# Attention with routed experts and a dense layer: who copies the transposed probabilities while 64-bit words are converted, and when the words are ordered

## Chip, core and metric

The kernel runs on one core of a Trainium2 chip. The metric is the device time of one execution in microseconds (us); the smaller the better. Engines: TensorE (PE, its weight loads PEld), VectorE (DVE), ScalarE (ACT), GpSimd (POOL), SyncE (SP), which only issues transfers here.

## What is computed

```python
# q, k, v: (2, 8, 768, 64); 16 cluster centroids per head
mask   = argmax(q_n @ c_n.T)[:, :, :, None] == argmax(k_n @ c_n.T)[:, :, None, :]
scores = where(mask, q @ k.T / 8, -1e9)
attn   = softmax(scores)                      # 768 x 768 per head, 16 heads
x      = (attn @ v) as rows of 1536 tokens x 512
e      = argmax(x @ w_gate + modality_bias[modality_id])     # 8 experts
x      = gate * (relu(x @ w1[e]) @ w2[e])     # 512 -> 1024 -> 512
out    = softplus(x @ w_in) @ w_out           # 512 -> 2048 -> 512
```

`w_in` and `w_out` arrive as float64, that is as pairs of 32-bit words; the kernel makes float32 of them itself.

## The kernel before

**Three stages.** Attention fills the first 300 us, the experts follow up to about 465 us, the dense layer (`g`, `o`) takes the rest. The change lies in the attention stage.

**Attention steps.** 16 heads of 6 row tiles make 96 steps, numbered `g`; the loop over `g` near line 1090 issues every step in the same order, and each engine works through its own instructions in that order. Step `g` is software-pipelined over three neighbours:

- `av_step(g)`: PE multiplies the transposed probabilities of the head before by `v` (tile `av`, L356).
- `S_mm(g+2)`: PE computes the scores of step g+2 (tile `S`, two buffers, L305 and L320); DVE takes their negated row maximum (`nm`, L322).
- `P_T(g)`: PE transposes the probabilities `P` of step g in six 128x128 blocks (L344) into two PSUM tiles `Tp` (i = 0 and 1; two buffers in all). Each `Tp` is copied to `PT` in SBUF: i = 1 always by ACT (L349), i = 0 by DVE (L347) or ACT.
- then the `jobs` of the step: loads (`load_raw`, `load_v`, `cv_load`), cluster masks (`sims_*`, tiles `sim`, `simT`, `mk`), the end of a head (`fin_x`, `fin_l`).
- `S_exp(g+2)`: ACT computes `P = exp(S + nm)` and its row sum (L331). This frees the `S` buffer.
- then the `after` work of the step (conversion, below), and a quarter of the split of a coming head's q and k (`prep_part`: ACT `kA` L278 and `qA` L283, DVE `kB` L281 and `qA` L286, POOL). `put_mask` sends mask rows into `qB` and `kB` by eight small transfers (L296).

**Conversion of the 64-bit words.** 16 pieces, j = 0 to 15, of 1 MB. `cvg[j] = 11 + (19*j)//4` is the step at which piece j begins: 11, 15, 20, 25, 30, 34, 39, 44, 49, 53, 58, 63, 68, 72, 77, 82. `cv_load(j)` (L439) brings the words into tile `words`, of which there are two buffers, so piece j can only land when piece j-2 has been read for the last time. At step cvg[j] ACT takes the absolute value of the high words (`cvd<-words`, L452); in the three steps behind it DVE does the rest: L454 and L455, then L460, then L464, which is the last reader of `words`. `cv_store(j)` (L470) writes the result to `w_rows` at step cvg[j]+4.

**SP's order.** All these transfers are issued by SP, one behind the other: a transfer that must wait for a buffer holds up those behind it. `load_raw` (L174, L175) brings q and k of a coming pair of heads and has to wait until DVE's `qA` of an earlier pair (L286) is done.

**What the diff touches:** the set `busy` (the three steps behind each cvg[j], 48 in all), the condition in `P_T`, and the step at which `cv_load` is issued.

```python
job(g0 - 4, cv_load, j)
for k in range(4):
    after.setdefault(g0 + k, []).append((cv_bits, (j, k)))
    if k:
        busy.add(g0 + k)
```

Of the kernel before, what the change touches and what calls it, by code (L numbers as in the profile page):

```python
# [32 lines left out]
def body(ctx, tc, qT, kT, vP, cen, mod, wg, bias, w1, w2, win, wout, out):  # L33
# [114 lines left out]
    desc = p_1.tile([128, 16], F32, name="desc")  # L148
    mk_a = p_1.tile([128, 1], F32, name="mk_a")
    mk_b = p_1.tile([128, 1], F32, name="mk_b")  # L150
    busy = set()
    raw, vt, sims, spl, mks, PT, P_t, S_t, nm_t, sums, av_t, xTu, rec, xb, lgT = ({} for _ in range(15))

    pend = []
# [181 lines left out]
    def P_T(g):  # L336
        h, t = divmod(g, NT)
        if t == 0:
            PT[h] = p_PT.tile([128, NT, S], F32, tag="PT", name="PT")
        P = P_t.pop(g)  # L340
        for i in range(2):
            ps = ps_T.tile([128, 3, 128], F32, tag="t", name="Tp")
            for j in range(3):
                pe.transpose(ps[:, j, :], P[:, i, j * 128:(j + 1) * 128], ident)  # L344
            dst = PT[h][:, 3 * i:3 * i + 3, t * 128:(t + 1) * 128]
            if i == 0 and g not in busy:
                dve.tensor_copy(dst, ps)  # L347
            else:
                act.copy(dst, ps)  # L349
# [595 lines left out]
    with tc.manual_schedule():  # L945
# [54 lines left out]
        def job(g, f, *a):  # L1000
            jobs.setdefault(g, []).append((f, a))
# [17 lines left out]
            job(6 * h + 14, fin_l, h)  # L1019
            job(6 * h + 15, fin_lT, h)  # L1020

        cvg = [11 + (19 * j) // 4 for j in range(16)]
        for j in range(16):
            g0 = cvg[j]
            job(g0 - 4, cv_load, j)
            for k in range(4):
                after.setdefault(g0 + k, []).append((cv_bits, (j, k)))
                if k:
                    busy.add(g0 + k)
            after.setdefault(g0 + 4, []).append((cv_store, (j,)))  # L1030

        e_t = p_1.tile([128, LROWS // 128 * LW], U32, name="empty")
# [60 lines left out]
        for g in range(NH * NT):  # L1093
            h, t = divmod(g, NT)
            if g > NT:
                av_step(g)
            S_mm(g + 2)
            P_T(g)
            for f, a in jobs.get(g, ()):
                if inspect.isgeneratorfunction(f):  # L1100
                    run(f, *a)
                else:
                    f(*a)
            S_exp(g + 2)
            drain()
            for f, a in after.get(g, ()):
                f(*a)
            h2, i2 = divmod(g - 3, NT)
            h2 += 2
            if 2 <= h2 < NH and i2 < 4:  # L1110
                prep_part(h2, i2)
                if i2 == 0 and h2 > 2:
                    put_mask(h2)
            if g == 8:
                put_mask(2)
# [64 lines left out]
        for i in range(1, LF + 1):  # L1180
            k = i - 1
# [13 lines left out]
        for x in seq:  # L1195
            kd, k, w, h = x
# [38 lines left out]
        for n in range(1, end):  # L1235
            kd, k, w, h = seq[n]
# [8 lines left out]
            while ks < len(halves) and at_load.get(halves[ks], end) < n + (n == 1):  # L1245
                k = halves[ks]
# [171 lines left out]
        for n in range(2, end):  # L1418
            kind, i, layer, s = seq[n]
# [153 lines left out]
        for c, y in enumerate((ys[NM - 1][1], ps_A.tile([128, 512], F32, tag="a", name="o"))):  # L1573
            cs = slice(c * 256, c * 256 + 256)
            for kt in range(16):
                gh, gl = gs[NM - 1, kt // 4]
                hi, lo = wts["out", kt // 2]
                a, k = (kt % 4) * 256 + 128, (kt % 2) * 512 + c * 256
# [50 lines left out]
```

## Time and profile before

| | |
|---|---|
| median of 3 runs | 746.4 us (745.55 to 747.06) |
| the profiled execution | 748.49 us, its span 746.8 us |
| busy over the span | PE 703.2, PEld 562.5, DVE 457.7, ACT 392.3, POOL 160.7 us |
| DMA | 100.18 MB, 134 GB/s on average |

The span is what the trace covers, and all times in trace rows count from its start; the remaining 1.7 us lie around it. Busy time is the sum of an engine's instructions; a row of the timeline gives the start, the duration, the engine, the line, the tile written `<-` the tiles read, and in brackets for how long the engine had been idle and what released it.

### The profile page before, as it was taken

How to read it: one execution, taken by the hardware profiler on the slowest of the kernel's cores; microseconds unless marked ns; L12 is line 12 of the kernel's file. 1: busy time of each engine (PE TensorE's matmuls, PEld its weight loads, DVE VectorE, ACT ScalarE, POOL GpSimd, SP SyncE). 2: the span in 40 equal slices, each digit the busy share in tenths (PEclk: the TensorE clock that was granted, in tenths of full speed). 3: DMA queues.
4: the chain of work that ended last, by engine and by line, in shares of the span. 5: the costliest groups of instructions: out<-in, count | busy, mean ns of one | idle time of the engine just before them, and what ended most of it. 6: DMA issues, size and time to landing. Idle time of an engine off the chain costs nothing. (4 is left out here: it accounts for less than half of the span.)

```text
span 746.8 us, 11746 instructions
## 1 busy us (share of the span) xinstructions
PE 703.2 (94%) x4498; PEld 562.5 (75%) x4498; DVE 457.7 (61%) x668; ACT 392.3 (53%) x635; POOL 160.7 (22%) x172
## 2 busy tenths in 40 slices
PE   4898999899888999999999999989999999999998
PEld 2665665556455655888898878989889899899887
DVE  4898998799799985865747446684423424323220
ACT  3777886787687876344645535542332332322320
POOL 4501120111231203664362431260000000000000
PEclk9999999999999999999999999999999999999999
DMA  4407354534534525769868964301000100000000
GB/s 136 148 17 257 112 208 145 204 135 160 201 123 145 178 104 183 250 227 397 324 228 310 411 216 168 128 1 29 26 18 15 37 7 29 1 1 29 1 29 28
DMA packets 38683, 100.18 MB, mean 134 GB/s; under 512 B 7934, under 2 KB 15486, under 8 KB 36576
## 3 DMA queue, kind: packets, MB, share of 16 engines
q1 hardware_dynamic: 35888, 92.22, 35.3%
q0 software_dynamic: 2592, 6.79, 2.6%
q8 instruction: 36, 0.59, 0.3%
q10 hardware_dynamic: 144, 0.39, 0.2%
q14 instruction: 23, 0.19, 0.1%
HBM read 79.13 MB, written 19.17 MB: 132 GB/s over the span
## 5 line engine op out<-in xcount | busy, mean ns | idle before, releaser
L1508 DVE SCALAR_TENSOR_TENSOR sp<-g,sp 128x1024 f32<-128x1024 f32 x24 | 29.4, 1224 | 149.7 <-ACT sp L1507 149.7
L1497 PE MATMUL g<-xh,wh 128*128 128x256 f32 x384 | 109.1, 284 | 0.0
L1497 PE MATMUL g<-xl,wh 128*128 128x256 f32 x384 | 108.1, 281 | 0.0
L1497 PE MATMUL g<-xh,wl 128*128 128x256 f32 x384 | 108.0, 281 | 0.0
L331 ACT ACTIVATE P<-S,nm 128x768 f32<-128x768 f32 x96 | 87.0, 906 | 38.8 <-DVE nm L322 34.7
L344 PE MATMUL Tp<-ident,P 128*128 128x128 f32 x576 | 84.7, 280 | 15.3 <-ACT PT L349 9.7
L1505 ACT ACTIVATE sp<-g 128x1024 f32<-128x1024 f32 x24 | 24.6, 1027 | 137.5 <-PE g L1497 127.6
L322 DVE TENSOR_REDUCE nm<-S 128x1 f32<-128x768 f32 x96 | 90.7, 946 | 9.1 <-PE S L320 8.7
L344 PEld LDWEIGHTS Tp<-ident,P 128*128 128x128 f32 x576 | 68.0, 142 | 28.5 <-ACT PT L349 15.2
L742 POOL TENSOR_TENSOR wl<-raw,wh 128x1024 fp32r<-128x1024 f32 x22 | 54.2, 2475 | 131.1 <-ACT wh L741 124.1
L356 PE MATMUL av<-PT,v 128*64 128x384 f32 x384 | 78.9, 506 | 0.0
L742 DVE TENSOR_TENSOR wl<-raw,wh 128x1024 fp32r<-128x1024 f32 x50 | 66.1, 1362 | 13.1 <-ACT wh L741 13.1
L741 ACT CAST wh<-raw 128x1024 fp32r<-128x1024 f32 x69 | 69.0, 1050 | 9.8 <-DMA raw<-in_w 7.2
L1497 PEld LDWEIGHTS g<-xl,wh 128*128 128x128 f32 x384 | 73.5, 191 | 0.5
L1497 PEld LDWEIGHTS g<-xh,wh 128*128 128x128 f32 x384 | 73.4, 191 | 0.5
L1497 PEld LDWEIGHTS g<-xh,wl 128*128 128x128 f32 x384 | 73.3, 191 | 0.0
L349 ACT COPY PT<-Tp 128x384 f32<-128x384 f32 x144 | 64.2, 483 | 14.9 <-PE Tp L344 14.1
L1532 PE MATMUL o<-wh,gT 128*128 128x512 f32 x216 | 69.7, 394 | 0.0
L305 PEld LDWEIGHTS S<-kA,qA 128*128 128x128 f32 x192 | 29.9, 195 | 50.2 <-ACT P L331 13.9
L305 PE MATMUL S<-kA,qA 128*128 128x384 f32 x192 | 60.6, 399 | 4.2 <-ACT P L331 3.8
L844 PE MATMUL y<-wh,hT 128*128 128x512 f32 x192 | 63.1, 398 | 0.0
L819 PE MATMUL h<-xh,wh 128*128 128x256 f32 x192 | 55.0, 287 | 0.5 <-DVEq L1350 0.5
(284 smaller groups left out, 1403.9 us busy)
## 6 DMA issues: line engine op xcount, KB each, us to landing
raw<-in_w SPq DMA_DIRECT2D x56, 512.0 KB, 7.5
words<-in_win SPq DMA_DIRECT2D x8, 1024.0 KB, 5.5
w_rows<-cvt SPq DMA_DIRECT2D x16, 512.0 KB, 3.2
words<-in_wout SPq DMA_DIRECT2D x8, 1024.0 KB, 6.5
whole<-in_w SPq DMA_DIRECT2D x16, 512.0 KB, 6.9
raw<-w_rows SPq DMA_DIRECT2D x16, 512.0 KB, 5.0
rawq<-in_qT SPq DMA_DIRECT2D x8, 384.0 KB, 3.6
v<-in_vP SPq DMA_DIRECT2D x8, 384.0 KB, 4.7
```

Source lines behind the costliest of these rows:

```text
L305: pe.matmul(ps[:, i, :HS], qA[:, t * 128:t * 128 + 128], kA[:, i * HS:(i + 1) * HS], start=True, stop=False)
L322: dve.tensor_reduce(out=nm_t[g], in_=ps[:, :, :HS], axis=AX.XY, op=ALU.max, negate=True)
L331: act.activation(out=P_t[g], in_=S_t.pop(g)[:, :, :HS], func=AF.Exp, bias=nm_t.pop(g), scale=1.0, accum_out=sums[h][:, t:t + 1],)
L344: pe.transpose(ps[:, j, :], P[:, i, j * 128:(j + 1) * 128], ident)
L349: act.copy(dst, ps)
L356: pe.matmul(av_t[h][64 * a:64 * a + 64, :], vt[p][:, kt, 64 * i:64 * i + 64], PT[h][:, kt, a * HS:(a + 1) * HS], start=(kt == 0), stop=(kt ...
L741: cp(self.hi, self.raw)
L742: eng.tensor_tensor(out=self.lo, in0=self.raw, in1=self.hi.bitcast(F32), op=ALU.subtract)
L819: pe.matmul(o, a, b[:, kt, :], start=(n == 0 and f % 2 == 0), stop=(n == 11), skip_group_check=True)
L844: pe.matmul(u["y"][j], x, y, start=(kt == 0 and i == 0), stop=(kt == 7 and i == 2))
L1497: pe.matmul(o, a, b[:, kt, :], start=(n == 0 and f % 2 == 0), stop=(n == 11), skip_group_check=True)
L1532: pe.matmul(ys[u][j], x[:, a:a + 128], y, start=(kt == 0 and i == 0), stop=(kt == 15 and i == 2))
```

## The change

While any piece is converted, from step 11 to step 85, ACT makes both copies of a step; before, DVE made the i = 0 copy in those steps of this range that were not in `busy`. And `cv_load(j)` is issued at step cvg[j]-6 and no longer at cvg[j]-4.

```diff
-    busy = set()
+    cvg = [11 + (19 * j) // 4 for j in range(16)]
...
-            if i == 0 and g not in busy:
+            if i == 0 and not cvg[0] <= g <= cvg[-1] + 3:
                 dve.tensor_copy(dst, ps)
             else:
                 act.copy(dst, ps)
...
-        cvg = [11 + (19 * j) // 4 for j in range(16)]
         for j in range(16):
             g0 = cvg[j]
-            job(g0 - 4, cv_load, j)
+            job(g0 - 6, cv_load, j)
             for k in range(4):
                 after.setdefault(g0 + k, []).append((cv_bits, (j, k)))
-                if k:
-                    busy.add(g0 + k)
```

SP's order around piece 6, before: the words of piece 6 stand behind `load_raw` of a pair of heads, and those of piece 7 behind the masks (a number behind a name tells one buffer from the next; `words_1390` is piece 6, `words_1536` piece 7).

```order
L296 DMA qB_1323<-mk_1082 16x384 x2
L296 DMA kB_1324<-mk_1082 16x384 x2
L470 DMA w_rows<-cvt_1225 128x1024
L174 DMA rawq_1386<-in_qT 128x768
L175 DMA rawk_1387<-in_kT 128x768
L439 DMA words_1390<-in_win 128x2048
L470 DMA w_rows<-cvt_1357 128x1024
L296 DMA qB_1504<-mk_1473 16x384 x2
L296 DMA kB_1505<-mk_1473 16x384 x2
L439 DMA words_1536<-in_win 128x2048
```

And in the changed kernel (`words_1306` is piece 6, `words_1475` piece 7):

```order
L439 DMA words_1306<-in_win 128x2048
L296 DMA qB_1325<-mk_1084 16x384 x2
L296 DMA kB_1326<-mk_1084 16x384 x2
L470 DMA w_rows<-cvt_1225 128x1024
L174 DMA rawq_1388<-in_qT 128x768
L175 DMA rawk_1389<-in_kT 128x768
L439 DMA words_1475<-in_win 128x2048
L470 DMA w_rows<-cvt_1359 128x1024
```

Piece 6 has moved ahead of four masks, a store and `load_raw`; piece 7 ahead of a store and four masks, and it stays behind `load_raw`. Pieces 1 and 11 move past a `load_raw` as piece 6 does.

ACT's order at steps 38 to 41, where piece 6 begins at step 39, before:

```order
L349 COPY PT_1405<-Tp_1492 128x3x128
L331 ACTIVATE P_1497,sums_1352<-S_1480,nm_1485 128x768
L452 ACTIVATE cvd_1499<-words_1390 128x1024
L278 CAST kA_1503<-rawk_997 64x768
L349 COPY PT_1405<-Tp_1521 128x3x128
L349 COPY PT_1405<-Tp_1526 128x3x128
L331 ACTIVATE P_1539,sums_1538<-S_1514,nm_1519 128x768
L192 COPY sim_1541<-misc_1531 128x384
L363 COPY xTu_1550<-av_1426 128x384
```

And in the changed kernel:

```order
L349 COPY PT_1405<-Tp_1489 128x3x128
L349 COPY PT_1405<-Tp_1494 128x3x128
L331 ACTIVATE P_1499,sums_1354<-S_1482,nm_1487 128x768
L452 ACTIVATE cvd_1501<-words_1306 128x1024
L278 CAST kA_1505<-rawk_997 64x768
L349 COPY PT_1405<-Tp_1523 128x3x128
L349 COPY PT_1405<-Tp_1528 128x3x128
L331 ACTIVATE P_1539,sums_1538<-S_1516,nm_1521 128x768
L192 COPY sim_1541<-misc_1533 128x384
L363 COPY xTu_1550<-av_1426 128x384
```

One copy more stands in front of the exponential of that step, and so in front of the absolute value (L452). DVE loses the copy that stood behind its row maximum of the same step. This happens at 27 steps: the 16 steps cvg[j], and 11 steps cvg[j]+4, where the next piece begins five steps after this one.

## Rows read from the trace of the kernel before

In a row of busy times stand the stretch and its length, the busy us (and instructions) of PE, PEld, DVE, ACT and POOL, the granted clock, the DMA share and GB/s.

**Rows 1.** Busy time by engine from 48 to 278 us, steps 11 to 90.
```profile
48.00:278.00 230.00, 209.72 (x1275) 135.34 (x1273) 205.35 (x333) 178.75 (x363) 41.79 (x45) 0.99 0.47 160
```

**Rows 2.** Waits of PE, 48 to 278 us: total us, times, longest us.
```profile
PE Tp L344 <- ACT PT L349: 9.7, 11, 2.5
...
PE misc L212 <- ACT sim L192: 2.1, 3, 0.7
```

**Rows 3.** Waits of ACT, 48 to 278 us.
```profile
ACT P L331 <- DVE nm L322: 27.8, 34, 1.8
...
ACT cvd L452 <- DMA words<-in_win: 6.7, 2, 4.4
ACT cvd L452 <- DMA words<-in_wout: 4.1, 1, 4.1
```

**Rows 4.** Timeline around the beginning of piece 6.
```profile
122.43 0.34 SPq L174 DMA_DIRECT2D rawq<-in_qT  x1
...
123.30 0.42 SPq L439 DMA_DIRECT2D words<-in_win  x1
...
128.10 0.20 ACT L331 ACTIVATION_READ_ACCUMULATOR P<-S,nm 128x1 f32 x1
...
132.67 1.12 ACT L452 ACTIVATE cvd<-words 128x1024 f32<-128x1024 f32 x1 [4.37 <-DMA words<-in_win]
...
134.93 0.92 PE L344 MATMUL Tp<-ident,P 128*128 128x128 f32 x6 [2.55 <-ACT PT L349]
```

**Rows 5.** Timeline around the beginning of piece 1.
```profile
55.06 0.43 SPq L439 DMA_DIRECT2D words<-in_win  x1
...
63.04 1.13 ACT L452 ACTIVATE cvd<-words 128x1024 f32<-128x1024 f32 x1 [2.35 <-DMA words<-in_win]
...
65.32 0.93 PE L344 MATMUL Tp<-ident,P 128*128 128x128 f32 x6 [1.21 <-ACT PT L349]
```

**Rows 6.** Timeline around the beginning of piece 11.
```profile
193.87 0.43 SPq L439 DMA_DIRECT2D words<-in_wout  x1
...
203.41 1.12 ACT L452 ACTIVATE cvd<-words 128x1024 f32<-128x1024 f32 x1 [4.07 <-DMA words<-in_wout]
...
205.66 0.92 PE L344 MATMUL Tp<-ident,P 128*128 128x128 f32 x6 [2.29 <-ACT PT L349]
```

**Rows 7.** The stretch behind piece 6's wait, columns as in rows 1.
```profile
136.53:139.95 3.42, 3.39 (x14) 3.30 (x15) 2.80 (x3) 3.42 (x8) 0.00 (x0) 0.50 0.01 4
```

**Rows 8.** Timeline: what the words of pieces 1, 6 and 11 stand behind after the change.
```profile
36.16 1.21 SPq L296 DMA_DIRECT2D kB<-mk  x2
...
112.34 1.22 DVE L464 SCALAR_TENSOR_TENSOR cvt<-words,cvt 128x1024 int32<-128x1024 int32 x1
...
179.13 1.22 DVE L464 SCALAR_TENSOR_TENSOR cvt<-words,cvt 128x1024 int32<-128x1024 int32 x1
```

**Rows 9.** Masks that come to stand behind piece 6, and the first scores that read them.
```profile
109.11 1.15 SPq L296 DMA_DIRECT2D qB<-mk  x2
...
128.08 0.51 PE L320 MATMUL S<-kB,qB 80*128 80x384 f32 x2
```

**Rows 10.** The copies, 48 to 278 us, by line: busy us, mean ns, idle before.
```profile
L349 ACT COPY PT<-Tp 128x384 f32<-128x384 f32 x128 | 56.6, 483 | 8.1 <-PE Tp L344 7.5
...
L347 DVE COPY PT<-Tp 128x384 f32<-128x384 f32 x32 | 17.4, 545 | 0.0
```

**Rows 11.** Timeline: two transposes that wait for a copy on DVE.
```profile
214.71 0.55 DVE L347 COPY PT<-Tp 128x384 f32<-128x384 f32 x1
...
215.31 0.55 PE L344 MATMUL Tp<-ident,P 128*128 128x128 f32 x3 [0.71 <-DVE PT L347]
...
242.46 0.55 DVE L347 COPY PT<-Tp 128x384 f32<-128x384 f32 x1
...
243.06 0.55 PE L344 MATMUL Tp<-ident,P 128*128 128x128 f32 x3 [0.90 <-DVE pm L614]
```

**Rows 12.** Busy time in the experts' stage, columns as in rows 1.
```profile
375.00:400.00 25.00, 25.00 (x184) 22.98 (x183) 12.81 (x13) 12.48 (x15) 9.90 (x13) 1.00 0.77 280
```

## Prediction

> **What bounds the kernel now.** I read the busy times of the stage that the change touches first, then who waits for whom in it, then the timeline at the longest waits.
>
> From 48 to 278 us PE is busy for 209.72 of 230.00 us, DVE for 205.35 and ACT for 178.75 [rows 1]. So PE sets the pace, DVE is close behind, and all that any change of the other engines can win here is PE's idle time, 20.3 us, plus what a lower clock costs. The later stages are PE's alone, with 25.00 busy of 25.00 us in the experts [rows 12]; the work in them is ordered behind the attention steps, loads included, so I take it that what the attention saves reaches the end, and that nothing is lost or won there.
>
> Where does PE's idle time come from? Its largest item is the transposes' wait for a copy on ACT: 9.7 us in 11 waits [rows 2]. But a copy is short, and a wait of 2.5 us cannot be its own length. ACT's own waits show two kinds: 34 short ones for DVE's row maximum, 27.8 us in all, and three long ones for the words, 6.7 and 4.1 us [rows 3]. The timeline joins the two: at pieces 1, 6 and 11 ACT sits idle for 2.35, 4.37 and 4.07 us in front of the absolute value because the words have not landed, the copies queued behind it are late, and PE's next transposes wait 1.21, 2.55 and 2.29 us [rows 4 to 6]. Right behind them comes PE's wait for `sim`, which ACT also makes late: 0.7 us, three times in the stage [rows 2].
>
> The second stall costs more than its idle time. Behind it the granted clock is 0.50, the lower of the two levels (1.2 instead of 2.4 GHz), for 3.42 us, with PE busy for 3.39 of them [rows 7].
>
> Why these three? Their words leave SP at 55.06, 123.30 and 193.87 us and are used 8.0, 9.4 and 9.5 us later, the moment they are there [rows 4 to 6]. All three are issued right behind `load_raw` (122.43 us for piece 6 [rows 4]), which waits for a buffer and then shares the DMA engines with them.
>
> **The words, two steps sooner.** "Two steps" is not what SP sees: there are two buffers, so a piece cannot be ordered before DVE's last read of the piece two before. What counts is what it now stands ahead of.
> - Piece 6: the last read of piece 4 ends at 112.34 + 1.22 = 113.56 us [rows 8], so the words leave then, not at 123.30. With the 9.4 us of now they land at 123.0; ACT wants them at 128.30 [rows 4], and 5 us are to spare.
> - Piece 11: free at 179.13 + 1.22 = 180.35 us [rows 8], landed by 189.9, wanted at 203.41 - 4.07 = 199.34 [rows 6].
> - Piece 1: its buffer is fresh, and it leaves behind the masks that end at 36.16 + 1.21 = 37.37 us [rows 8]; landed by 46, wanted at 60.69 [rows 5].
> - The other 13 pieces have no wait now, and most gain a few us at best; I count nothing.
>
> What this saves: 1.21 + 2.55 + 2.29 = 6.05 us of transposes' waits, 2.1 us of waits for `sim`, and half of 3.42 us of low clock, 1.7 us. Together **9.9 us**. Something stays: ACT is fullest at just these three steps (absolute value, `kA`, two copies, exponential, `sim`). I estimate 0.3 us each, between nothing and the 0.7 of the `sim` waits: **-0.9 us**.
>
> What is queued behind the words' new wait on SP: for piece 6, four masks that now leave at 109.11 us and will leave near 114; the first scores that read them run at 128.08 us [rows 9], so 14 us are left. The store behind it has a buffer of its own to spare. `load_raw` waits for its buffer until 122.43 us anyway [rows 4]. I cost these at nothing; the cover is those 14 us.
>
> **The copies.** 27 of them leave DVE, at 545 ns each 14.7 us, and come to ACT, at 483 ns each 13.0 us [rows 10]. Little of either lies on the path:
> - What DVE gives up counts where PE waits behind a DVE copy. Two such places stand out: 0.71 us at 215.31, and 0.90 us at 243.06, where the copy that began at 242.46 had just ended [rows 11]. Both copies are among the 27 (steps 67 and 77: four steps behind the start of piece 11, and the first of piece 14). At both, ACT is idle meanwhile, waiting for the row maximum. I take 1.6 us. Elsewhere an earlier row maximum starts the exponential earlier; bounds are nothing and all the rest of PE's idle time, 20.3 - 8.2 - 1.6 = 10.5 us. I take 0.5 us, near the lower end: where I followed the queues, DVE's time was lost again in front of the absolute value, which ACT does no sooner.
> - What ACT takes on counts where it has no idle time in front of an absolute value. Bounds: nothing, and 16 steps x 0.48 = 7.7 us. ACT's waits for the row maximum, 27.8 us in 34 places [rows 3], and its idle time of 51 us in the stage [rows 1] lie mostly in the steps that get a copy more. I take nothing.
>
> So the copies bring **2.1 us**, between -7.7 and 12.1.
>
> **The sum.** 748.5 (profiled execution) - 9.9 + 0.9 - 2.1 = 737.4 us. That execution lay 2.1 us above the median of the runs, so against the median: **735.3 us**, 1.5% less. About 0.2%, 1.5 us, is what a measurement of this kernel can tell from no change.
>
> **Rivals.**
> 1. *DVE is the bound, not PE.* Then each copy that leaves it counts. For: ACT waits for DVE 34 times [rows 3], and DVE is busy for 89% of the stage [rows 1]. Against: PE's busy time leaves only 20.3 us. With the words' gain and all of the rest of PE's idle time: 746.4 - 9.9 - 1.6 - 10.5 = 724.4 us. The Trainium skill ("Perfetto Trace Analysis", Identifying the Most-Contended Engine) speaks for this rival: it says that the busy share of matmuls is not a good measure for TensorE, that the share of weight loads is to be used in its place, and that the engine with the highest occupancy is to be relieved first. By that rule PE stands at 135.34 of 230 us [rows 1], DVE leads, and its 14.7 us would come off besides the words: 746.4 - 9.9 - 14.7 = 721.8 us. The trace bears it out in part only: over whole stretches PE's matmuls follow each other without a gap [rows 12]. Chance 12%.
> 2. *ACT's queue takes the place of the words.* At each of the 16 steps cvg[j] an extra copy stands in front of the exponential and the absolute value, and so of the next step's copies, for which PE waits. Half of the bound of 7.7 us, without the 2.1 us from DVE, gives 746.4 - 9.0 + 3.9 = 741.3 us: 11%. If all 27 copies lie on the path, it decides: 746.4 - 9.0 + 13.0 = 750.4 us, slower than before. The point is reached when the copies cost more than the words' 9.0 us, that is when 19 or more of the 27 are uncovered. Against: adding 13.0 us leaves ACT 51.2 - 10.8 - 13.0 = 27 us idle. 5%.
> 3. *The words come no sooner.* If SP reaches them as late as now, or if they share the DMA engines with something else, the change does not do what it says, and only the copies are left: 746.4 - 2.1 = 744.3 us, within a us of no change if the copies do nothing either. Against: SP's order in the changed kernel. 8%.
>
> **How the numbers follow.** My forecast, 731 to 740 us, has 64%, rival 1 12%, rival 2 16% (11 and 5), rival 3 8%. The range from 728 to 742 us takes in the forecast's own bounds, the milder half of rival 2 and the upper part of rival 1; outside lie most of rival 1, the hard half of rival 2 and rival 3. Faster by over 0.2%, below 744.9 us: the forecast, rival 1, the milder rival 2 and half of rival 3, less a little for what I have not seen: 0.89. Within 0.2%: the other half of rival 3 and a rest: 0.06. Slower: 0.05.
>
> **What would show it.** Right: the three waits of ACT for the words are gone; the granted clock is 1.00 in all of the attention stage; SP issues piece 6 near 113 us and piece 11 some 3 us sooner than 180; DVE has 27 copies less, its busy time in the stage falls by about 15 us and ACT's rises by 13; the stage ends 10 to 12 us sooner, and the rest of the page is as before, only shifted. Wrong: ACT still waits for words; or PE's waits for copies on ACT are as long as before with no wait of ACT in front of them (rival 2); or PE's idle time in the stage falls below 5 us (rival 1).

## The result and the profile after

The changed kernel takes 733.65 us (median of 4 runs, 732.19 to 734.55) against 746.62 us (745.55 to 747.06) of the kernel before: a ratio of 0.9827, 95% interval 0.9806 to 0.9847, or 13.0 us less. The forecast was 735.3 us, its range 728 to 742. The profiled execution took 733.08 us, with a span of 731.3 us, against 746.8 before.

The stage first, by the same view and an equally long stretch as [rows 1], 10 us earlier; the columns are the same.

```profile
38.00:268.00 230.00, 218.59 (x1357) 143.88 (x1356) 205.97 (x328) 197.31 (x410) 42.94 (x47) 1.00 0.52 164
```

PE is busy for 218.59 us of 230 and no longer 209.72. DVE shows nearly the same busy time as before, because the same 230 us now hold more steps. The clock reads 1.00.

Now the waits of PE and then of ACT in this stretch (total us, times, longest us), for [rows 2] and [rows 3].

```profile
PE Tp L344 <- ACT PT L349: 4.5, 9, 0.8
PE S L305 <- ACT P L331: 3.3, 4, 1.0
PE misc L386 <- ACT simT L217: 1.5, 5, 0.7
PE Tp L344 <- DVE PT L347: 1.2, 1, 1.2
```

```profile
ACT P L331 <- DVE nm L322: 20.4, 24, 2.2
ACT PT L349 <- PE Tp L344: 5.7, 10, 1.0
```

PE's waits for ACT's copies have fallen from 9.7 to 4.5 us, and the longest is 0.8 us. ACT's lines for the words are gone; its waits for the row maximum are fewer.

Piece 6 in the timeline, for [rows 4]:

```profile
110.16 0.33 SPq L439 DMA_DIRECT2D words<-in_win  x1
...
118.11 0.33 SPq L174 DMA_DIRECT2D rawq<-in_qT  x1
...
123.21 0.92 ACT L331 ACTIVATE P<-S,nm 128x768 f32<-128x768 f32 x1
...
124.10 1.16 ACT L452 ACTIVATE cvd<-words 128x1024 f32<-128x1024 f32 x1
...
126.60 0.93 ACT L331 ACTIVATE P<-S,nm 128x768 f32<-128x768 f32 x1
...
130.48 0.55 PE L386 MATMUL misc<-ident,xTu 128*128 128x128 f32 x3 [0.20 <-ACT simT L217]
```

The words leave 8 us ahead of `load_raw`, and the absolute value follows the exponential with no idle time. From that exponential to the next ACT takes 126.60 - 123.21 = 3.39 us; before, it was 135.15 - 127.31 = 7.84:

```profile
127.31 0.91 ACT L331 ACTIVATE P<-S,nm 128x768 f32<-128x768 f32 x1
...
135.15 0.90 ACT L331 ACTIVATE P<-S,nm 128x768 f32<-128x768 f32 x1
```

The whole difference by place, from the starts of the 96 exponentials (L331), each counted from the first one of its execution (they are numbered from 0, as the steps whose scores they take): the last comes 14.2 us sooner than before. 2.4, 4.5 and 4.2 us of that fall into the one step behind the start of pieces 1, 6 and 11, together 11.0 us; the other 3.2 us are spread over the rest. Behind the last exponential 460.5 us follow, before 461.1. So the gain stays to the end.

### The profile page after: what moved, and what is told of

Its sections match the earlier page's. It is cut to its first block, busy times and chain, and to the rows that moved or that the text cites. A ratio compares the mean times of both kernels' runs of the same rounds, so it can differ in the third digit from the quotient of the medians.

```text
span 731.3 us, 11746 instructions
## 1 busy us (share of the span) xinstructions
PE 697.8 (95%) x4498; PEld 561.3 (77%) x4498; DVE 446.6 (61%) x641; ACT 400.4 (55%) x662; POOL 161.7 (22%) x172
## 5 line engine op out<-in xcount | busy, mean ns | idle before, releaser
L331 ACT ACTIVATE P<-S,nm 128x768 f32<-128x768 f32 x96 | 87.3, 910 | 30.1 <-DVE nm L322 26.5
L344 PE MATMUL Tp<-ident,P 128*128 128x128 f32 x576 | 82.2, 277 | 8.2 <-ACT PT L349 4.5
L349 ACT COPY PT<-Tp 128x384 f32<-128x384 f32 x171 | 74.5, 484 | 11.7 <-PE Tp L344 10.3
```

Source lines behind the costliest of these rows:

```text
L331: act.activation(out=P_t[g], in_=S_t.pop(g)[:, :, :HS], func=AF.Exp, bias=nm_t.pop(g), scale=1.0, accum_out=sums[h][:, t:t + 1],)
```

## Experiments

All are timed against the kernel before on the same chip; a ratio below is to that kernel.

**The words alone.**

```diff
-            job(g0 - 4, cv_load, j)
+            job(g0 - 6, cv_load, j)
```

> Before, with the words ordered two steps sooner; DVE keeps its copies. Theory (three waits for words, copies nearly nothing): 9 to 11 us off the kernel before, so about 736.5 us (735 to 738), no wait of ACT for words, and PE clock 1.00 from 30 to 290 us. Rival (VectorE is the bound, and the words' waits only let it catch up): 3 to 6 us off, 741 to 743 us, because waits of ACT for the row maximum grow to replace those for words. Rival (the copies bring most): under 4 us off.

Measured: 737.53 us, ratio 0.9869 (0.9832 to 0.9905), 9.8 us off. No wait for words is left, and the last exponential comes 10.7 us sooner: the three steps give 11.0 us, and the first ten exponentials, which scatter from trace to trace, take 0.4 back. The theory holds, and the rival that has VectorE swallow the gain falls: ACT's waits for the row maximum are 28.4 us in 36 places here, as before.

**The copies alone.** The changed kernel with `job(g0 - 4, cv_load, j)`.

> Before, with all copies of steps 11 to 85 on ScalarE; the words stay at cvg[j]-4. Theory: about 2 us off (0 to 4), 743 to 746 us, and the three waits for words stay at 2 to 4.5 us each. Rival (VectorE is the bound): 8 us or more off. Rival (ScalarE's queue is the bound): slower than before, 748 us or more.

Measured: 743.41 us, ratio 0.9953 (0.9919 to 0.9987), 3.5 us off. ACT's timeline at piece 1:

```profile
54.94 0.43 SPq L439 DMA_DIRECT2D words<-in_win  x1
...
63.96 1.12 ACT L452 ACTIVATE cvd<-words 128x1024 f32<-128x1024 f32 x1 [3.41 <-DMA words<-in_win]
```

The three waits stay: 3.41, 4.18 and 3.01 us. At piece 1 the wait has even grown from 2.35 [rows 5]: ACT is ready for the words at 60.55 us, before at 60.69, but they are used 9.0 us after SP issued them and not 8.0. The last exponential comes 2.1 us sooner. Together the two parts give 9.8 + 3.5 = 13.3 us, and both at once 13.0: within the intervals, they add up.

**Only three pieces sooner.** The kernel before with

```diff
-            job(g0 - 4, cv_load, j)
+            job(g0 - (6 if j in (1, 6, 11) else 4), cv_load, j)
```

> Before, with only pieces 1, 6 and 11 ordered two steps sooner, the three that stand behind load_raw; DVE keeps its copies. Theory: the same as with all 16 sooner, within 1 us (735 to 738 us). Rival (the other 13 pieces gain too, through less crowding of the DMA engines): half of the gain or less, 740 us or more.

Measured: 736.85 us, ratio 0.9864 (0.9830 to 0.9899), the same as with all 16. The other 13 bring nothing that can be told.

**The words where they were, `load_raw` later.** The kernel before with

```diff
-                job(max(b - 13, 0), load_raw, p)
+                job(max(b - 13, 0) + (2 if p in (3, 5, 7) else 0), load_raw, p)
```

> Before, with the words where they were, but load_raw of pairs 3, 5 and 7 two steps later, so that on SP it stands behind the words of pieces 1, 6 and 11 instead of ahead of them; DVE keeps its copies. Theory (what hurts is the place behind load_raw, not the step): most of the gain comes back, 736 to 739 us, and the words of piece 6 leave within 2 us of the end of the masks before them. Rival (the words are simply ordered too late, whatever stands ahead): the waits for words stay over 2 us at pieces 6 and 11 and the time stays over 743 us.

Measured: 736.18 us, ratio 0.9845 (0.9809 to 0.9881): the whole gain of the words, and not one of them was issued at an earlier step. SP around piece 6:

```profile
108.15 1.22 SPq L296 DMA_DIRECT2D kB<-mk  x2
111.44 0.34 SPq L470 DMA_DIRECT2D w_rows<-cvt  x1
111.87 0.38 SPq L439 DMA_DIRECT2D words<-in_win  x1
120.28 0.33 SPq L174 DMA_DIRECT2D rawq<-in_qT  x1
```

The words leave at 111.87 us, right behind the store for which SP had to wait, and `load_raw` waits behind them until 120.28. So what hurt was the place behind `load_raw` on SP. That place delays the words in two ways, which no run separates: they are issued later, and they travel beside `load_raw`, which was issued just before. At piece 6 they were used 9.4 us after their issue [rows 4], while the median transfer of `words` from `in_win` in the kernel before lands 5.5 us after its issue. (The expectation's "within 2 us of the masks" is a miss by 0.5 us, 111.87 against 109.37: the store stands between.)

**All first copies back on VectorE, words early.** The changed kernel with `if i == 0:`.

> The changed kernel, but with every i = 0 copy on VectorE (75 copies of steps 11 to 85 back from ScalarE, 48 of them there already before). Measures what a VectorE copy costs once the words are on time. VectorE gets 75 x 0.545 = 41 us back on 206 us busy in a stage of about 215: theory (VectorE is close behind TensorE) 15 to 30 us slower than the changed kernel, 748 to 763 us. Rival (TensorE alone sets the pace and VectorE's time is hidden): under 5 us slower.

Measured: 755.95 us, ratio 1.0124 (1.0084 to 1.0164), 22 us over the changed kernel. The stage from 38 to 268 us (columns as in [rows 1]), and the waits of PE and of ACT in it:

```profile
38.00:268.00 230.00, 208.53 (x1241) 133.72 (x1240) 222.19 (x378) 160.32 (x308) 42.31 (x47) 0.98 0.49 153
```


```profile
PE Tp L344 <- DVE PT L347: 12.1, 13, 2.1
PE Tp L344 <- DVE pm L614: 3.2, 3, 1.9
```

```profile
ACT P L331 <- DVE nm L322: 49.5, 50, 2.9
```

Here VectorE is the bound, busy for 222.19 of 230 us while PE has fallen to 208.53. From this kernel to that with the words alone, 48 copies leave it and 18.4 us go, 0.38 us for each copy of 0.545 (some of it may be the clock, 0.98 here and 1.00 there); from there to the changed kernel 27 more leave and 3.9 us go, 0.14 each. One reading is that VectorE's price falls as TensorE's floor comes near. But the 48 also stand in other places, the steps in which DVE converts, and these runs do not separate the place of a copy from the order in which it left.

**Half of the moved copies.** First only the 16 of the steps cvg[j] on ScalarE (`if i == 0 and not (any(c <= g <= c + 3 for c in cvg))`), then only the 11 between pieces (`if i == 0 and (g in cvg or not cvg[0] <= g <= cvg[-1] + 3)`).

> The changed kernel, but only the 16 copies of the first steps of the pieces have moved to ScalarE (those in front of the absolute value); the 11 of the steps between pieces are back on VectorE. Theory: these 16 bring nothing, so the time is that of early words alone, 1 to 3 us over the changed kernel. Rival (ScalarE late in front of the absolute value costs): slower than early words alone by 2 us or more.

> The changed kernel, but only the 11 copies of the steps between pieces have moved; the 16 of the first steps are back on VectorE. Theory: these 11 bring about 1 us (step 67), so the time lies within 1 us of the changed kernel. Rival (the 16 first copies cost ScalarE time): faster than the changed kernel by 1 us or more.

Measured: 733.97 us, ratio 0.9822 (0.9784 to 0.9860), and 734.98 us, 0.9835 (0.9799 to 0.9870). Both lie within 1.4 us of the changed kernel, and their intervals overlap with that of the words alone. The traces tell more, if the time is counted from exponential 10, ahead of every moved copy: up to there the traces scatter, the two of the changed kernel by 0.6 us. From there to the last, against the words alone, the 16 bring 2.4 us, the 11 bring 1.8 us, and all 27 together 2.9 us (2.6 in the second trace of the changed kernel). So the theory fails for the first (the 16 do bring something) and is inconclusive for the second; the two halves bring more by themselves, 4.2 us, than together.

**All 96 on ScalarE.** The changed kernel with `if i == 0 and g < 0:`; then once more beside the changed kernel itself, and with the words two steps sooner again (`job(g0 - 8, cv_load, j)`).

> The changed kernel, with all 96 i = 0 copies on ScalarE, so also those of steps 0 to 10 and 86 to 95 (21 more). Those steps have no conversion, but at the end 2 waits of about 1 us each for a VectorE copy (near 262 and 268 us). Theory: 1 to 3 us faster than the changed kernel. Rival (ScalarE has the splits of expert weights there and becomes late): 1 us or more slower.

> The changed kernel once more, as the measure for the two beside it on the same chip: 732 to 735 us.

> All 96 first copies on ScalarE and the words two steps sooner, once more, beside the changed kernel. If its stage is shorter by what the traces showed, 1.3 us: 0.5 to 2 us faster than the changed kernel. If that was chance: within 0.5 us.

> As the kernel beside it with all copies on ScalarE, and the words ordered at cvg[j]-8, two steps sooner again. There are two buffers, so a piece cannot land before the last read of the piece two before it. Theory (no wait for words is left): the same time within 1 us. Rival (the words' wait for their buffer now stands on SP in front of masks and load_raw and holds them up): 2 us or more slower, with PE or ACT waiting for rawk, rawq, qB or kB.

Measured: 732.05 us, ratio 0.9786 (0.9749 to 0.9822); then, on one chip, 734.94 us for the changed kernel (0.9816, 0.9779 to 0.9854), 733.48 us with all copies on ScalarE (0.9788, 0.9750 to 0.9826) and 732.07 us with the words at cvg[j]-8 as well (0.9785, 0.9747 to 0.9823). All copies on ScalarE is 1.5 us faster side by side, and its last exponential came 1.3 us sooner in one trace against the changed kernel's and 1.7 us in the other pair; the intervals overlap, so I call it likely, not settled. It does not come where the expectation put it: in the first pair 0.6 of the 1.3 us and in the second all 1.7 lie in the first ten steps, and from exponential 86 to the last the kernel with all copies on ScalarE is 0.5 us slower. Ordering the words still sooner, 1.4 us faster here with overlapping intervals, changes nothing that can be told, in either direction: with no wait for words there is nothing to win, and no engine waits for the masks behind them.

## Why the prediction was right, point by point

- **What bounds the stage.** The three waits for words were the largest item, and the way they were said to reach PE is shown: words alone, three words alone, and `load_raw` moved out of the way give the same, 10 to 12 us by the times and 10.5 to 10.7 us by the last exponential.
- **The size of the words' term.** 9.0 us was forecast, 9.8 measured, 11.1 in the trace from exponential 10 on. The terms inside it were wrong, and partly cancelled, so that the total was nearer than its parts: that is luck. I counted PE's visible waits (8.2 us), added 1.7 us for the clock and took 0.9 us off for what ACT keeps. The trace of the words alone shows 2.4, 4.5 and 4.2 us at the three steps; ACT's own waits were 2.35, 4.37 and 4.07 [rows 4 to 6]. In the three steps behind each come 0.0, +0.5 and -0.4 us, and next to nothing anywhere else. It is the wait in ACT's full queue that comes back whole, not PE's idle time behind it.
- **The clock term** was too large: 1.7 us forecast, 0.5 to 0.9 us by the traces. These are the two steps from the first exponential behind the stall to the second after it, of the kernel before and then of the words alone (columns as in [rows 1]):

```profile
135.15:140.43 5.28, 4.57 (x24) 4.01 (x24) 4.16 (x8) 5.21 (x13) 0.00 (x0) 0.68 0.04 17
```

```profile
129.00:134.51 5.51, 5.31 (x37) 3.64 (x33) 5.08 (x9) 5.19 (x14) 0.00 (x0) 1.00 0.41 149
```

  With the mean clock at 0.68 the two steps took 5.28 us, with 1.00 they took 5.51. ACT is busy for 5.2 us in both, working off what had piled up: it set the pace there, and PE had time to run slowly. The cost comes one step later. Six transposes take 1.48 us at the low clock and 0.82 at the high one, PE falls behind, and ACT's copy in the next step waits 1.34 us for its transposes and not 0.64. First the kernel before, then the words alone:

```profile
138.54 1.48 PE L344 MATMUL Tp<-ident,P 128*128 128x128 f32 x6
...
142.77 0.48 ACT L349 COPY PT<-Tp 128x384 f32<-128x384 f32 x1 [1.34 <-PE Tp L344]
...
144.17 0.90 ACT L331 ACTIVATE P<-S,nm 128x768 f32<-128x768 f32 x1 [0.92 <-DVE nm L322]
```

```profile
132.20 0.82 PE L344 MATMUL Tp<-ident,P 128*128 128x128 f32 x6
...
136.16 0.48 ACT L349 COPY PT<-Tp 128x384 f32<-128x384 f32 x1 [0.64 <-PE Tp L344]
...
137.56 0.90 ACT L331 ACTIVATE P<-S,nm 128x768 f32<-128x768 f32 x1 [0.93 <-DVE nm L322]
```

  Over the three steps the kernel before takes 144.17 - 135.15 = 9.02 us and the words alone 137.56 - 129.00 = 8.56, so 0.46 us come back. Behind piece 11, where the clock was 1.00 before too, the kernel before makes the same three steps in 0.4 us less than the words alone; had it done so behind piece 6, the low clock would have cost 0.9 us there, which is an estimate. "Half of 3.42 us" took PE's busy time for time on the path.
- **What stays at the three steps:** 0.9 us estimated. In the changed kernel PE waits 0.20, 0.20 (at 130.48 above) and 0.71 us for `simT` behind pieces 1, 6 and 11, 1.1 us in all, the last at

```profile
196.02 0.55 PE L386 MATMUL misc<-ident,xTu 128*128 128x128 f32 x3 [0.71 <-ACT simT L217]
```

  The size was about right; but of the same wait 0.47 us stood before at pieces 1 and 11 each, so not all of it was left over from the stalls.
- **The copies.** 2.1 us forecast; timed, 3.9 us between the words alone and both, and 3.5 us by themselves, with an interval from 1 to 6 us. By the traces from exponential 10 on it is 2.9 us (2.6 in the second trace), and 2.6 by themselves. So the total was a little low, and its parts were wrong: I put 1.6 us on two places and 0.5 on "elsewhere an earlier row maximum". At step 77 nothing came: exponential 80, the next behind that copy's step, gains nothing over exponential 79 in any kernel in which the copy has moved; PE's wait of 0.90 us is gone, and behind the next absolute value PE waits 0.64 us where it had waited 0.18. At step 67 exponential 70 comes 0.5 us sooner in every kernel in which that copy has moved and in no other; but in the changed kernel exponential 69 comes 0.6 us later (0.3 in the second trace):

```profile
201.73 0.90 ACT L331 ACTIVATE P<-S,nm 128x768 f32<-128x768 f32 x1 [2.24 <-DVE nm L322]
...
202.78 0.61 PE L305 MATMUL S<-kA,qA 128*128 128x384 f32 x2 [0.70 <-ACT P L331]
```

  PE no longer waits for the copy there, but for the exponential, and that for the row maximum, which stands behind other work on DVE. The wait of 0.71 us [rows 11] has become one of 0.70. So the step that was mis-sized is "elsewhere": about 2 us came there, and I had taken 0.5, because I had followed the queues at a few places, where DVE's gain was lost again, and generalized.
- **What was costed at nothing** held: the masks behind piece 6 left at 110.59 us, no engine waited for them in the attention steps, and even at cvg[j]-8 nothing did.
- **Rival 1 (VectorE is the bound)** falls as stated: 14.7 us less on DVE brought 3.9 us. The Trainium skill ("Perfetto Trace Analysis", Identifying the Most-Contended Engine) says to judge TensorE's headroom by MFU (its share of the peak arithmetic rate) and the busy share of its weight loads, and to optimize the engine of highest occupancy first. That all 14.7 us would come off was the prediction's reading of it, by the weight loads alone, and the measurement decides against that here; with 75 copies more on VectorE, where it is shown to be the bound, relieving it does pay. **Rival 2** falls: PE's waits for copies on ACT other than the three stalls were 9.7 - 6.05 = 3.7 us before and are 4.5 us now, and all copies on ScalarE are no slower. One place stays open: in the three steps behind piece 11 the changed kernel takes 0.9 us longer than the words alone, in both traces. **Rival 3** falls with SP's issue times.
- **Signs named in advance:** most came, and their sizes were often off. No wait of ACT for words is left, and DVE has 21 copies where it had 48. Piece 6 was issued at 110.16 us (near 113 was named) and piece 11 at 170.66 (some 177). The last exponential comes 14.2 us sooner (10 to 12). From the first exponential to the last DVE is busy for 10.9 us less and ACT for 8.2 more (15 and 13): instructions of one engine overlap a little in the trace, so a copy adds less busy time than its length. And the granted clock is not 1.00 in all of the stage: it is 0.50 from 16.2 to 22.9 us, ahead of the first piece; the exponentials there come no later than before.

## What to carry to other kernels

A load that one issuing queue holds behind another load, which itself waits for a buffer, is late however early its step looks: look for the wait in the consumer's queue and then at what was issued just ahead of it, and swap the two. Size such a stall by the wait of the engine whose queue is full, not by the idle time seen further down, and count a slow clock only as far as the slowed engine then makes another one wait, here 0.5 to 0.9 us of 1.7. What work moved between two nearly full engines pays cannot be read from its length: here 48 copies were worth 0.38 us each, and the 27 others 0.14.

## What was not expected of the hardware

Stretches of about 3.4 us, now and then 6.7, at the lower of the two clock levels come and go between executions, even of the same program: the first trace of the changed kernel has one from 16.2 to 22.9 us, the second has none there and one near 217 us. In both one falls at the start of the dense layer; in the first:

```profile
487.10:490.50 3.40, 3.40 (x19) 3.40 (x18) 3.31 (x3) 2.04 (x3) 1.56 (x1) 0.50 0.35 82
```

The same place ran at full clock with the words alone. From the last exponential to the end the four executions without such a stretch there or later took 458.7 to 459.9 us, the seven with one at the dense layer 460.2 to 461.5 us, the two with one in the experts' stage 461.6 and 462.4 us. These are different kernels, one trace each but for the changed one, so the costs are only likely: about 1 to 3 us for a stretch of low clock in the later stages, against the 0.5 to 0.9 us behind piece 6, where ScalarE had work piled up. What sets its place was not tried.
